# Decode attention, four layers: V15's second half in a bank of its own, wo columns ahead of V15, wq of layers 2 and 3 in 1, 2, 2 rows

## The chip, the cores and the metric

The kernel runs on one core of a Trainium2 chip. The metric is the device time of one launch in microseconds (us), lower is better. A profile shows one execution; its span leaves out about 1.8 us of the launch, so a span of 1984.0 us belongs to a time of 1985.8 us.

## The reference, cut to what matters

Four layers, blocks A, B, A, B. Each normalises a vector of 640, projects it with wq (640 x 6144) to 32 heads of 192, attends over a cache of 8192 keys, projects with wo and adds the result to the vector. One query only, so every byte of the caches and weights is used once in a layer (layers 0 and 2 share theirs, and so do 1 and 3).

```python
    x = x + _A_ref(_layernorm(x, axis=-1), A_k_cache, A_v_cache, A_wq, A_wo)
    x = x + _B_ref(_layernorm(x, axis=-1), B_k_cache, B_v_cache, B_wq, B_wo)
    x = x + _A_ref(_layernorm(x, axis=-1), A_k_cache, A_v_cache, A_wq, A_wo)
    x = x + _B_ref(_layernorm(x, axis=-1), B_k_cache, B_v_cache, B_wq, B_wo)
# within a block: q = x @ wq; scores = q.k / sqrt(192); p = softmax; o = p @ v; out = o @ wo
```

## The kernel before

Heads go in 16 pairs per layer. K and V of a pair are 12.6 MB between them, and SBUF holds eight slots of 3.15 MB. For K, DVE multiplies the tile by the query and PE sums over the head dimension with the identity; for V, PE multiplies by the probabilities and DVE picks the wanted parts out of PSUM. A transfer into a slot is issued when the last reader of that slot is done. V15 stands for the V tile of the last pair of a layer, whichever pair that is.

The parts the change touches: which slices of wq come in which piece, how many of wo's 15 columns come late (`NB`, one number per layer), the order of the steps at a layer's end, and the V product.

```python
    Q_PARTS = [(0, 2), (2, 2), (4, 1)]        # first row and number of rows of each piece of wq
    NB = [0, 5, 0, 5]                         # wo columns that come after V15
    # ... (cut)
            steps.append(("e", l, p - 1))
            steps += [("v", l, p, 0), ("wc", l, 2)] if NB[l] else [("wc", l, 2), ("v", l, p, 0)]
            steps += [("wo", l, 2), ("v", l, p, 1)]
            if NB[l]:
                plan.append(("vq", l))
                both(("wob", l))
            steps.append(("e", l, p))
            both(("wol", l))
```

Here "v" is the V product, "e" the picks, "wc" the turning of 15 columns of the attention output, "wo" and "wob" the projections with the early and the late columns of wo, "wol" the last pair's projection, and "vq" the transfer of V15's last quarter. V15 has 2 keys per PSUM group, so that 2 picks instead of 8 follow it:

```python
                k = 2 if p == NPAIR - 1 else VK   # VK = 8
                # ... (cut)
                for i in range(2 if end else VK):
                    e = DV.op(lambda v, i=i: (
                        v.tensor_scalar(acc[:], O[:, 0:DH], pick[:, 0:1], None, ALU.mult) if i == 0 else
                        v.scalar_tensor_tensor(out=acc[:], in0=O[:, i * DH:(i + 1) * DH], scalar=pick[:, i:i + 1], in1=acc[:],
                                               op0=ALU.mult, op1=ALU.add)), e if i else None, bank=Ou)
```

In the step into layer 2 the slots chain: wq's third piece takes the slot of wq's first piece, and layer 2's first V half takes the slot of the first half of K0, which was kept since layer 0. So V is issued when PE has summed that K half, and that needs layer 2's first query.

## Time and profile before

| | before |
|---|---|
| median of the first 3 runs | 1985.51 us (1985.11 to 1985.80) |
| span of the profiled execution | 1984.0 us |
| bytes moved | 849.25 MB |
| slice 21 of 40 (the step into layer 2) | 388 GB/s |
| last slice | 353 GB/s |

How to read it: with transfers busy all the time, only places where the DMA engines stand still, and what follows the last transfer, can be won.

Besides the views, the trace records when each of a transfer's sixteen parts landed, and when each packet started and how long it took. "Landing" below means the last of the sixteen parts, and "spread" the distance from the first part to the last.

### The profile page before, as it was taken

Reading aid. Unit: us, or ns where it says so; the run is one execution under the profiler, and the core shown is the slowest. Engines: PE = TensorE matmul, PEld = TensorE weight load, DVE = VectorE, ACT = ScalarE, POOL = GpSimd, SP = SyncE. Lnnn points to the kernel's source line nnn. Section 1 sums busy time; section 2 is a strip of 40 time slices with the busy share of each in tenths; the row PEclk is TensorE's granted clock in tenths of the full one; section 3 lists DMA queues with packets and bytes.
Section 4 is the critical chain, followed back from the end, with each engine's and each line's share of the span. In section 5 each row is a group of like instructions: output and inputs, shape, how many; then the busy total and the mean of one; then the engine's idle time right before and its main releaser. Section 6 shows DMA issues by size and latency. Waiting matters only on the chain.

```text
span 1984.0 us, 13908 instructions
## 1 busy us (share of the span) xinstructions
PE 1273.4 (64%) x8310; PEld 150.1 (8%) x3266; DVE 1200.7 (61%) x1371; ACT 139.5 (7%) x461; POOL 4.5 (0%) x22
## 2 busy tenths in 40 slices
PE   3567567566466666665775665675676766656657
PEld 0001001000200100100020010010002001001001
DVE  3566467467166656556745565665664775665665
ACT  0000000000000000000010000000000000000000
POOL 0000000000000000000000000000000000000000
PEclk9787777777587787777876777878886887777777
DMA  9999999999999999999999999999999999999998
GB/s 412 438 430 431 431 437 429 431 430 431 433 435 431 432 429 436 430 431 432 427 388 433 430 430 430 432 430 430 431 431 427 435 432 434 430 432 432 432 431 353
DMA packets 26926, 849.25 MB, mean 428 GB/s; under 512 B 3184, under 2 KB 3184, under 8 KB 3952
## 3 DMA queue, kind: packets, MB, share of 16 engines
q1 hardware_dynamic: 26720, 848.38, 99.5%
q8 instruction: 45, 0.74, 0.2%
q14 instruction: 17, 0.14, 0.0%
q10 hardware_dynamic: 144, 0.00, 0.0%
HBM read 848.36 MB, written 0.00 MB: 428 GB/s over the span
## 4 chain that ended last, share of the span: by engine, by line
DMA 68%; DVE 15%; PE 15%; ACT 1%; issue 0%; SPq 0%
DMA pool<-in_B_k_cache_dram 27%; DMA pool<-in_A_v_cache_dram 20%; DMA pool<-in_A_k_cache_dram 14%; DVE pool L543 13%; PE S L58 6%; PE OY L58 5%; DMA pool<-in_B_v_cache_dram 4%; PE OY L620 3%; DMA pool<-in_B_wo_dram 2%; ACT p_sb L580 1%; DVE acc L639 1%; DMA pool<-in_A_wq_dram 1%; DVE s_sb L565 1%; PE OY L513 0%; PE S L556 0%
## 5 line engine op out<-in xcount | busy, mean ns | idle before, releaser
L543 DVE TENSOR_TENSOR pool<-pool,q_sb 128x3072 bf16<-128x3072 bf16 x512 | 861.2, 1753 | 241.5 <-DMA pool<-in_B_k_cache_dram 144.0
L58 PE MATMUL S<-pool,ident 128*128 128x512 bf16 x2944 | 789.1, 425 | 20.3 <-DVE pool L543 19.0
L650 PE MATMUL TB<-acc,small 128*1 128x192 f32 x240 | 82.1, 493 | 219.1 <-DVE acc L639 219.1
L556 PE MATMUL S<-pool,ident 128*128 128x512 bf16 x128 | 62.9, 491 | 213.6 <-DVE pool L543 213.6
L58 PE MATMUL OY<-pool,p_sb 128*16 128x512 bf16 x1920 | 197.0, 485 | 0.0
L638 DVE TENSOR_SCALAR acc<-OY,small 128x192 f32<-128x192 f32 x64 | 26.7, 418 | 274.2 <-PE OY L58 246.2
L620 PE MATMUL OY<-pool,p_sb 128*16 128x512 bf16 (+1 forms) x1216 | 147.5, 497 | 62.7 <-DMA pool<-in_A_v_cache_dram 56.4
L639 DVE SCALAR_TENSOR_TENSOR acc<-OY,small,acc 128x192 f32<-128x192 f32 x424 | 177.1, 418 | 14.9
L565 DVE TENSOR_REDUCE s_sb<-S 128x64 f32<-128x512 f32 x128 | 88.1, 688 | 69.4 <-PE S L58 69.4
L502 ACT ACTIVATE q_sb<-QM 128x192 bf16<-128x192 f32 x60 | 19.9, 331 | 954.8 <-PE QM L496 954.8
L661 ACT ACTIVATE rows<-TB,small 1x192 bf16<-1x192 f32 x120 | 43.2, 406 | 585.1 <-PE TB L650 585.1
L634 DVE RECIPROCAL small<-TB 1x2 f32<-1x2 f32 x64 | 11.2, 175 | 96.7 <-PE TB L595 75.2
L580 ACT ACTIVATE p_sb<-s_sb,small 64x128 bf16<-64x128 f32 x128 | 55.7, 435 | 161.9 <-DVE small L574 161.1
L556 PEld LDWEIGHTS S<-pool,ident 128*128 128x128 bf16 x128 | 13.0, 101 | 686.2 <-DVE pool L543 636.4
L595 PE MATMUL TB<-small,ones 128*1 128x2 f32 x120 | 11.4, 165 | 74.1 <-ACT p_sb L580 74.1
L620 PEld LDWEIGHTS OY<-pool,p_sb 128*16 128x16 bf16 (+1 forms) x1216 | 39.3, 107 | 203.6 <-issue 133.5
L570 PE MATMUL QM<-ident,m_bf 128*64 128x64 bf16 x128 | 14.1, 217 | 54.4 <-DVE m_bf L567 53.8
L650 PEld LDWEIGHTS TB<-acc,small 128*1 128x1 f32 x240 | 19.7, 101 | 311.4 <-DVE acc L639 283.9
L513 PE MATMUL OY<-oT,pool 128*128 128x1 bf16 x900 | 38.2, 178 | 3.5 <-ACT oT L528 2.8
L513 PEld LDWEIGHTS OY<-oT,pool 128*128 128x128 bf16 x900 | 37.1, 131 | 7.0 <-ACT oT L528 3.6
L574 DVE TENSOR_REDUCE small<-QM 128x1 f32<-128x64 f32 x64 | 14.4, 225 | 36.1 <-PE QM L570 36.1
L496 PEld LDWEIGHTS QM<-rows,one_b 1*64 1x64 bf16 x120 | 6.2, 100 | 350.7 <-issue 344.8
(59 smaller groups left out, 186.1 us busy)
## 6 DMA issues: line engine op xcount, KB each, us to landing
pool<-in_B_k_cache_dram SPq DMA_DIRECT2D x28, 6144.0 KB, 38.1
pool<-in_B_v_cache_dram SPq DMA_DIRECT2D x28, 6144.0 KB, 34.2
pool<-in_A_v_cache_dram SPq DMA_DIRECT2D x27, 6144.0 KB, 27.6
pool<-in_A_k_cache_dram SPq DMA_DIRECT2D x34, 3072.0 KB, 20.4
pool<-in_A_k_cache_dram SPq DMA_DIRECT2D x14, 6144.0 KB, 36.8
pool<-in_A_v_cache_dram SPq DMA_DIRECT2D x10, 3072.0 KB, 14.3
pool<-in_B_k_cache_dram SPq DMA_DIRECT2D x8, 3072.0 KB, 22.7
pool<-in_A_wo_dram SPq DMA_DIRECT2D x6, 2400.0 KB, 21.4
```

Of the source, the lines that this page charges most:

```text
L58: return t.add_instruction(mybir.InstMatmult(name=t.bass.get_next_instruction_name(), engine=mybir.EngineType.PE, ins=[t.lower_ap(rhs), t. ...
L502: lambda a: a.activation(q_sb[i][:], QM[:, 0:DH], ACT.Copy), e, last["q"][i], bank=QMu)
L513: e = PE.op(lambda t, i=i, c=c, f=y_first[0], fin=n[0] == "wol" and i == k - 1: t.matmul(YB[:, c:c + 1], lhsT=t3[:, i, c:D:DC], rhs=o[:, i ...
L543: e = DV.op(lambda v, d0=d0: v.tensor_tensor(k3[:, :, d0:d0 + QD], kin[:, :, d0:d0 + QD], q_sb[qi][:, d0:d0 + QD].unsqueeze(1).broadcast_t ...
L556: t.matmul(S[:, :], lhsT=ident[:], rhs=k3[:, :, d0:d0 + R], start=True, stop=fin) if d0 == 0 else
L565: lambda v, u=u: v.tensor_reduce(s[:, u * JU:(u + 1) * JU], SP_[u][:].rearrange("p (j r) -> p j r", r=R), AX.X, ALU.add), ev_S[p, u], last ...
L580: ev_p[p] = AC.op(lambda a, h=h, r=r: a.activation(p_sb[par][r, :, h], s[r, :], ACT.Exp, bias=negm[par][r, 0:1], accum_out=l_col[par][r, h ...
L620: t.matmul(o, lhsT=x, rhs=y, start=f, stop=fin) if c == 0 else
L638: v.tensor_scalar(acc[:], O[:, 0:DH], pick[:, 0:1], None, ALU.mult) if i == 0 else
L639: v.scalar_tensor_tensor(out=acc[:], in0=O[:, i * DH:(i + 1) * DH], scalar=pick[:, i:i + 1], in1=acc[:], op0=ALU.mult, op1=ALU.add)), e if ...
L650: e = PE.op(lambda t, h=h: t.matmul(TB[96:97, C_O + h * DH:C_O + (h + 1) * DH], lhsT=half[:, h:h + 1], rhs=acc[:], start=True, stop=True), ...
L661: last["TO"] = last["row_written"] = AC.op(lambda a, h=h: a.activation(orow[:, o0 + h * DH:o0 + (h + 1) * DH], TB[96:97, C_O + h * DH:C_O ...
```

## The change

The intent: at the end of layers 1 and 3, let V15's first half be summed and picked (8 keys per group) while the second half is still on its way, and put the second half into the free scores bank with 2 keys per group, so that only two picks follow it; turn the output's columns before V15, not in its middle; bring fewer wo columns late; and issue wq in pieces that give its first slot back sooner. The first query's copy also goes from ACT to DVE.

```diff
-    Q_PARTS = [(0, 2), (2, 2), (4, 1)]
+    Q_PARTS = [[(0, 2), (2, 2), (4, 1)] if l < 2 else [(0, 1), (1, 2), (3, 2)] for l in range(NL)]
-    NB = [0, 5, 0, 5]
+    NB = [0, 0, 0, 3]
+    SPLIT = (1, 3)
...
-            steps += [("v", l, p, 0), ("wc", l, 2)] if NB[l] else [("wc", l, 2), ("v", l, p, 0)]
-            steps += [("wo", l, 2), ("v", l, p, 1)]
+            steps.append(("wc", l, 2))
+            if l in SPLIT:
+                steps += [("v", l, p, 0), ("e", l, p, 0), ("wo", l, 2), ("v", l, p, 1)]
+                plan.append(("vq", l))
+            else:
+                steps += [("wo", l, 2), ("v", l, p)]
...
-            ev_q[0] = last["QB"] = AC.op(
-                lambda a: a.activation(q_sb[i0][:], QM[:, 0:DH], ACT.Copy, scale=rs[:, 0:1]),
+            ev_q[0] = last["QB"] = DV.op(
+                lambda v: v.tensor_scalar(q_sb[i0][:], QM[:, 0:DH], rs[:, 0:1], None, ALU.mult),
...
-                k = 2 if p == NPAIR - 1 else VK
+                k, B, Bu = (2, SP_[0], Su[0]) if part == 1 else (VK, O, Ou)
...
+                for i in range(2 if part == 1 else VK):
                     e = DV.op(lambda v, i=i: (
-                        v.tensor_scalar(acc[:], O[:, 0:DH], pick[:, 0:1], None, ALU.mult) if i == 0 else
-                        v.scalar_tensor_tensor(out=acc[:], in0=O[:, i * DH:(i + 1) * DH], ...
+                        v.tensor_scalar(acc[:], O[:, 0:DH], pick[:, 0:1], None, ALU.mult) if i == 0 and part != 1 else
+                        v.scalar_tensor_tensor(out=acc[:], in0=B[:, i * DH:(i + 1) * DH], ...
```

The cuts leave out how the events and slot releases of the two halves are kept apart.

More of the change, by code (lines that the diff above doesn't have):

```diff
@@ L265, in build @@
             steps.append(("e", l, p - 1))
-            steps += [("v", l, p, 0), ("wc", l, 2)] if NB[l] else [("wc", l, 2), ("v", l, p, 0)]
-            steps += [("wo", l, 2), ("v", l, p, 1)]
+            steps.append(("wc", l, 2))
[4 more added lines that the diff above has]
+                steps += [("wo", l, 2), ("v", l, p)]
             if NB[l]:
-                plan.append(("vq", l))
                 both(("wob", l))
@@ L280, in released @@
                     l, p = l + 2, ORDER[l + 2]["pairs"].index(pair(l, p))
-                return at[("v", l, p, 1) if n[0] == "v" and p == NPAIR - 1 else ("v", l, p) if n[0] == "v" else ("m", l, p, n[3])]
+                return at[("v", l, p, n[3]) if n[0] == "v" and p == NPAIR - 1 and l in SPLIT else ("v", l, p) if n[0] == "v" else ("m", l, p, n[3])]
             return at[("wob", n[1]) if n[0] == "wo" and n[2] == 2 and NB[n[1]] else n]
@@ L325, in wq_rows @@
         def wq_rows(l, g):
-            c0, k = Q_PARTS[g]
+            c0, k = Q_PARTS[l][g]
             if l < 2:
@@ L333, in quarters @@
         def quarters(n):
-            return n[0] == "v" and n[2:] == (NPAIR - 1, 1) and NB[n[1]] > 0
+            return n[0] == "v" and n[2:] == (NPAIR - 1, 1) and n[1] in SPLIT
         def transfer(n):
@@ L374, in transfer @@
             elif n[0] == "wq":
-                c0, k = Q_PARTS[n[2]]
+                c0, k = Q_PARTS[l][n[2]]
                 f = lambda s: s.dma_start(
@@ L405, in build @@
                     lc=[None, None], S=[None, None], O=ev_zero)
-        for k in "MX QB rows qbc TT TO YB orow oT oTl acc rl xb rs st stt row_written".split():
+        for k in "MX QB rows qbc TT TO YB orow oT oTl acc rl xb rs st stt sel row_written".split():
             last[k] = None
@@ L469, in q_rows @@
                 n = ("wq", l, g)
-                c0, k = Q_PARTS[g]
+                c0, k = Q_PARTS[l][g]
                 t3 = wq_rows(l, g)[:, :, ORDER[l]["q1"] * PD if l < 2 else 0:]
@@ L583, in softmax, with values @@
                 last["s"][par] = last["negm"][par] = ev_p[p]
-            def values(p, us=(0, 1)):
+            def values(p, part=None):
                 par = (l * NPAIR + p) % 2
                 nl, np_ = first_load("v", l, p)
-                k = 2 if p == NPAIR - 1 else VK
-                N = min(512, k * DH)
                 PE.wait(ev_p[p])
-                if 0 in us:
+                if part != 1:
                     PE.wait(last["rl"])
@@ L602, in values @@
                     last["lc"][par] = ev_l[p] = e
-                PE.wait(last["O"])
-                rounds = J // k // G
-                for r in range(us[0] * rounds // 2, (us[-1] + 1) * rounds // 2):
-                    u, i = divmod(r, rounds // 2)
-                    u = turn[nl, np_][u]
+                k, B, Bu = (2, SP_[0], Su[0]) if part == 1 else (VK, O, Ou)
+                PE.wait(last["S"][0] if part == 1 else last["O"])
+                N = min(512, k * DH)
+                groups = []
+                for u in (turn[nl, np_] if part is None else (part,)):
+                    groups += [(u, j) for j in range(0, JU, k)]
+                n = len(groups)
+                for r in range(0, n, G):
+                    u, j = groups[r]
                     PE.wait(need(("v", nl, np_, u)))
+                    if part == 1 and j >= JU // 2:
+                        PE.wait(need(("vq", l)))
                     t = slot[place[("v", nl, np_, u)]]
-                    if p == NPAIR - 1 and i == rounds // 4 and quarters(("v", nl, np_, u)):
-                        PE.wait(need(("vq", l)))
                     for c in range(k * DH // N):
                         for g in range(G):
-                            j = (i * G + g) * k
-                            o, x, y = (O[32 * g:32 * g + 2 * k, c * N:(c + 1) * N],
+                            u, j = groups[r + g]
+                            o, x, y = (B[32 * g:32 * g + 2 * k, c * N:(c + 1) * N],
                                        p_sb[par][:, u * JU + j:u * JU + j + k, :].rearrange("p j h -> p (j h)"),
                                        t[:, j * DH + c * N:j * DH + (c + 1) * N])
-                            f, fin = r == 0, r == rounds - 1
+                            f, fin = r == 0, r == n - G
                             e = PE.op(lambda t, c=c, g=g, o=o, x=x, y=y, f=f, fin=fin: (
@@ L621, in values @@
                                 matmul_held(t, o, x, y, f, fin, 32, 32 * g)),
-                                signal=(fin and c == k * DH // N - 1 and g == G - 1), bank=Ou)
-                if 1 not in us:
-                    return
-                ev_O[p] = last["p"][par] = e
+                                signal=(fin and c == k * DH // N - 1 and g == G - 1), bank=Bu)
+                ev_O[p, part] = last["p"][par] = e
                 if not stays("v", l, p):
-                    for u in range(2):
+                    for u in ((0, 1) if part is None else (part,)):
@@ L628, in values, with select @@
                         freed[("v", nl, np_, u)] = e
+            def select(p, part=None):
+                end = p == NPAIR - 1
+                a, n = (slice(0, P), 1) if end else (slice(96, 97), 2)
+                if part != 1:
+                    last["rl"] = DV.op(lambda v: v.reciprocal(rl[a, 0:n], TB[a, C_L:C_L + n]), ev_l[p], last["TO"], bank=TBu)
+                DV.wait(ev_O[p, part], last["acc"], ev_pick)
+                e = None
+                B, Bu = (SP_[0], Su[0]) if part == 1 else (O, Ou)
+                for i in range(2 if part == 1 else VK):
+                    e = DV.op(lambda v, i=i: (
+                        v.tensor_scalar(acc[:], O[:, 0:DH], pick[:, 0:1], None, ALU.mult) if i == 0 and part != 1 else
+                        v.scalar_tensor_tensor(out=acc[:], in0=B[:, i * DH:(i + 1) * DH], scalar=pick[:, i:i + 1], in1=acc[:],
+                                               op0=ALU.mult, op1=ALU.add)), e or last["sel"], bank=Bu)
+                if part == 1:
+                    last["S"][0] = e
+                else:
+                    last["O"] = e
+                last["sel"] = e
+                return e
@@ L630, in gather @@
             def gather(p):
                 end = p == NPAIR - 1
-                a, n = (slice(0, P), 1) if end else (slice(96, 97), 2)
-                ev_rl = last["rl"] = DV.op(lambda v: v.reciprocal(rl[a, 0:n], TB[a, C_L:C_L + n]), ev_l[p], last["TO"], bank=TBu)
-                DV.wait(ev_O[p], last["acc"], ev_pick)
-                for i in range(2 if end else VK):
-                    e = DV.op(lambda v, i=i: (
-                        v.tensor_scalar(acc[:], O[:, 0:DH], pick[:, 0:1], None, ALU.mult) if i == 0 else
-                        v.scalar_tensor_tensor(out=acc[:], in0=O[:, i * DH:(i + 1) * DH], scalar=pick[:, i:i + 1], in1=acc[:],
-                                               op0=ALU.mult, op1=ALU.add)), e if i else None, bank=Ou)
@@ L641, in gather @@
-                last["O"] = e
+                e = select(p, 1 if end and l in SPLIT else None)
+                ev_rl = last["rl"]
                 PE.wait(e, last["TO"], last["TT"])
@@ L671, in layer @@
                 elif n[0] == "v":
-                    values(n[2], n[3:] or (0, 1))
+                    values(*n[2:])
                 elif n[0] == "e":
-                    gather(n[2])
+                    (select if n[3:] else gather)(*n[2:])
                 elif n[0] == "wq":
```

## The prediction

> **What bounds the kernel now.** I read the page's 40 slices first, then its chain by engine, then the chain in order of time, then the busy shares of short stretches around the two places where the slices dip.
>
> ```profile
> DMA  9999999999999999999999999999999999999998
> GB/s 412 438 430 431 431 437 429 431 430 431 433 435 431 432 429 436 430 431 432 427 388 433 430 430 430 432 430 430 431 431 427 435 432 434 430 432 432 432 431 353
> DMA packets 26926, 849.25 MB, mean 428 GB/s; under 512 B 3184, under 2 KB 3184, under 8 KB 3952
> ...
> DMA 68%; DVE 15%; PE 15%; ACT 1%; issue 0%; SPq 0%
> ```
>
> The transfers are busy in every slice, while PE and DVE are busy 64% and 61% of the span and hide behind them. In the undisturbed parts the trace moves 433 GB/s; 849.25 MB at that rate is 1961.3 us of a span of 1984.0. The change loads the same bytes. So everything any schedule could win is 22.7 us, 1.1%: **faster by 2% (39.7 us) is out of reach**. Two slices dip: number 21 (388, the step from layer 1 to layer 2) and the last (353, the end). Slice 21 lacks 45/433 x 49.6 = 5.2 us. Those are where the change works.
>
> How much of the dip counts? Each transfer lands in sixteen parts, one per DMA engine, and the trace has their landings. The first of the sixteen parts comes well before the last, and the distance grows: 1.25 us at 22 us, 3.8 us at 500 us, 6.5 us at 1002.85. Only the last part releases a consumer. So what counts is the engine that lags. While the fifteen others idle ahead of it, nothing is lost. From the last landings, with 7.30 us for a half tile of 3.15 MB (the usual distance):
>
> - 1002.85 first half of V15, 1006.54 and 1010.20 its second half, 1012.14 the late wo columns, 1013.32 the last wo rows, 1020.24 and 1027.14 wq with two rows each, 1030.59 wq with one row. All these distances are bytes over rate: the lagging engine never stops, though the slices dip around 1006 and 1024.
> - The next landing, the first V half of layer 2, is at 1039.25: 8.66 us after 1030.59 for a transfer of 7.30 us. **Here even the slowest engine stands still, 1.36 us.** Its first part lands at 1038.69, so all sixteen started together: all had been empty.
>
> ```profile
> 1022.00:1024.00 2.00, 2.00 (x17) 0.10 (x1) 2.00 (x2) 0.00 (x0) 0.00 (x0) 0.50 0.84 357
> 1024.00:1026.00 2.00, 2.00 (x9) 0.00 (x0) 2.00 (x2) 0.00 (x0) 0.00 (x0) 0.77 0.83 265
> 1026.00:1028.00 2.00, 2.00 (x11) 0.00 (x0) 2.00 (x2) 0.00 (x0) 0.00 (x0) 1.00 1.04 444
> 1028.00:1030.00 2.00, 2.00 (x17) 0.09 (x3) 2.00 (x2) 0.00 (x0) 0.00 (x0) 1.00 0.37 156
> ```
>
> Columns: stretch, length, busy PE, PE loads, DVE, ACT, POOL, granted PE clock, DMA share, GB/s. Only the last stretch is a real stop. The transfer that ends it was held back:
>
> ```profile
> 1007.03 16.99 SPq L376 DMA_DIRECT2D pool<-in_A_wq_dram  x3
> 1029.60 0.34 SPq L371 DMA_DIRECT2D pool<-in_A_v_cache_dram  x1
> ```
>
> The queue issues wq's three pieces from 1007.03 to 1024, then V at 1029.60, since V takes the place of K0's first half, whose products end only then: PE was in the queries of wq's first piece from 1020.28 to 1023.65, because that piece landed at 1020.24.
>
> The end of the span:
>
> ```profile
> 1937.57 40.13 DMA pool<-in_B_wo_dram
> 1977.70 0.05 issue
> 1977.74 1.16 PE OY L513 x25
> 1978.90 0.99 PE TB L646 x12
> 1979.89 0.02 issue
> 1979.91 0.28 ACT oTl L656
> 1980.19 0.04 issue
> 1980.23 0.77 PE OY L513 x15
> 1981.01 0.02 issue
> 1981.03 0.16 DVE x_bf L696
> ```
>
> The late wo columns land at 1977.70, 25 projections follow, then the turn of the last pair, its projection and the output. Beside it, DVE's second pick ended at about 1978.46: two paths within 0.4 us.
>
> **What the Trainium skill says.** "DMA: Bandwidth & Descriptors", section "Why a DMA increments its semaphore by 16 and not by 1": a transfer runs on up to sixteen engines that finish independently, and only the full count means landed. The trace agrees (spread up to 6.5 us). The same page, "Where 436 GB/s comes from", gives a ceiling of 435.2 GB/s; the trace's 433 leaves nothing to win in rate. "Runtime: NRT & Kernel Launch", "Instruction fetch mechanics": instructions come in blocks of 16 KiB through a DMA queue of their own. The trace has packets of 16384 B of about 1.05 us each, and the spread grows in steps of about 1 us; one more or fewer on the lagging engine is my noise. "TensorE: Matmul & The Clock Gate", "What's actually happening": the clock is halved until about 3.4 us of activity; here it is 0.50 until 1024 and 1.00 from 1026, some 5 us after PE resumed.
>
> **The change part by part.** The slots that every transfer gets come out the same when I follow both allotments; only release times move.
>
> 1. *wo whole in layer 1, ahead of V15.* The 5 late columns (1.94 us) move before V15; bytes equal. V15's last quarter lands at 1012.14 instead of 1010.20. After it: half of 32 products of 2.73 us, 1.37; two picks of 0.42 and hops, 0.95; so the turn of the last pair starts at 1014.45, against 1013.27. It **costs 1.2 us** on the path into layer 2: first query at 1019.75 instead of 1018.57 (its copy goes from ACT, 0.42 us, to DVE, about the same).
> 2. *wo columns ahead of V15.* The 15 column products (1.07 us) follow ACT's rows at 1001.8, not V15's first half: the last wo rows and wq are issued near 1003, 3.7 us earlier. wq's second piece, waiting on the wo slot, goes at 1010.6 instead of about 1013. This fills the leading engines only.
> 3. *wq in 1, 2, 2 rows.* The first piece lands at 1016.75 instead of 1020.24, before the state is normalised; its queries take half of 3.3 us, from 1019.3 to 1020.9. The third piece, which needs that slot, goes at 1020.9 instead of about 1023.7 and keeps the lagging engine busy until 1030.5. K0's first products are then bound by DVE: four chunks of 1.68 us from 1019.75, and 1.46 for the last six matmuls, 1028.0. **V is issued at 1028.0 instead of 1029.60, 1.6 us earlier.** Issue to slowest landing was 9.65 us, less 7.30 of transfer: 2.35 of fixed delay. So it could flow at 1030.35, with the engine free at 1030.5: the stop of 1.36 us closes, by a margin of about 0.2.
> 4. *V15's halves.* The first half with 8 keys per group is 24 matmuls of 512 columns instead of 32 of 384, 2.56 us at half clock instead of 2.73. Its 8 picks (0.42 + 3.14 us from the trace) lie beside wo's projection and the wait for the second half. The second half stays at 32 matmuls and 2 picks. Layers 0 and 2 take 8 keys throughout, 6 more picks, 2.6 us, at layer ends that have over 10 us of transfers issued ahead (landings there show no stop). Nothing on the path.
> 5. *The end.* wo with 12 columns delays V15 by 0.8 us: its last quarter lands at 1976.55, not 1975.77. PE is free in time now, where before it came 0.4 us late from the projection. Matmuls to 1977.95, picks to 1978.9, the turn at 1978.9 instead of 1978.83. wo's 3 columns, landed at 1977.7, need 0.7 and are done at 1978.65. **About +0.1 us.**
>
> Sum: -1.36 + 0.1 = -1.3 us. I add nothing for fewer PE instructions (about 190 of 11,576, under one fetch).
>
> **The rivals.**
> - *All of slice 21 comes back* (gaps at 1006, 1024 and 1029, some 4.9 us): then 1980.5. For it, the GB/s row; against it, the lagging engine, which shows no idle in the first two. It would need the lag to be harmless.
> - *The stop stays:* the clock rises later, or 1.2 us from part 1 eats the 1.6, and V is issued at 1029 or later. Then 0.4 to 1.3 us of it remain, 1984.5 to 1985.6. For it: a margin of 0.2 us. Against: PE begins 1 us earlier too.
> - *The tail gains:* the split takes picks off the path and ends 1 us earlier, 1983. Against it: two picks stay behind the last landing.
> - *The later layers lose,* by 6 more picks. DVE is off the path there; nothing.
>
> **Range and chances.** 1985.5 - 1.3 = 1984.2. From 1982.3 (a further 1 to 2 us from a fetch or the tail) to 1985.6 (nothing closes). Faster by over 2%: 0.003; within 2%: 0.994; slower: 0.003.
>
> **What would show it.** The distance between the landings of wq's third piece and of the first V half of layer 2 should fall from 8.66 to about 7.3 us; V's issue should come about 1.6 us earlier against wq's last landing; slice 21 should rise above 400 GB/s; the chain at the end should pass through a pick or the last quarter of V15 and not through 25 wo matmuls, with 7.5 us from the landing of V15's last quarter to the end of the span in place of 8.2. I am wrong if the whole dip comes back as time, or the tail moves by over 1 us.

## More of the kernel before

The instruction fetches are a queue of their own on the page. The lines are kind, packets, MB and share of the sixteen engines' span.

```profile
q1 hardware_dynamic: 26720, 848.38, 99.5%
q8 instruction: 45, 0.74, 0.2%
```

## The result, and the profile after

The changed kernel took **1986.89 us** (median of 4 runs, 1985.87 to 1988.34) against 1985.65 us before (4 runs). The ratio is 1.0007, with a 95% interval of 0.9990 to 1.0024: the same within 2%, but above the predicted range and on the other side of the kernel before. A ratio here is the mean time of one kernel's fast runs over the mean of the other's fast runs of the same rounds, so it isn't quite the ratio of the medians.

The page of the changed kernel, in the same rows as before (transfers, rate, packets, chain by engine):

```profile
DMA  9999999999999999999999999999999999999997
GB/s 412 436 432 429 430 437 429 430 437 425 434 436 430 429 435 432 429 432 435 425 398 438 423 420 431 431 427 430 434 429 427 436 428 434 433 432 433 431 434 340
DMA packets 26782, 849.25 MB, mean 428 GB/s; under 512 B 3168, under 2 KB 3168, under 8 KB 3808
...
DMA 65%; PE 17%; DVE 16%; ACT 1%; issue 0%; SPq 0%
```

Slice 21 went from 388 to 398 only, not above 400, and the two slices after it fell from 433 and 430 to 423 and 420. The second trace of the same kernel (again, below) has 396 for slice 21 and 431 and 432 after it, so only the first of these is the kernel's own. The stretches of the step into layer 2 (same columns as in the prediction; DMA share and GB/s are the last two):

```profile
1020.00:1022.00 2.00, 1.38 (x9) 0.10 (x1) 2.00 (x2) 0.00 (x0) 0.00 (x0) 0.50 0.71 230
1022.00:1024.00 2.00, 2.00 (x7) 0.00 (x0) 2.00 (x2) 0.00 (x0) 0.00 (x0) 0.50 0.95 380
...
1028.00:1030.00 2.00, 2.00 (x27) 0.27 (x7) 2.00 (x2) 0.00 (x0) 0.00 (x0) 1.00 1.13 388
1030.00:1032.00 2.00, 2.00 (x11) 0.00 (x0) 2.00 (x2) 0.00 (x0) 0.00 (x0) 1.00 0.90 369
1032.00:1034.00 2.00, 2.00 (x11) 0.00 (x0) 1.19 (x2) 0.00 (x0) 0.00 (x0) 1.00 0.95 406
```

The same in the kernel before, from 1030 on:

```profile
1030.00:1032.00 2.00, 2.00 (x25) 0.19 (x4) 2.00 (x3) 0.00 (x0) 0.00 (x0) 1.00 0.78 209
1032.00:1034.00 2.00, 2.00 (x11) 0.00 (x0) 0.61 (x2) 0.00 (x0) 0.00 (x0) 1.00 1.06 455
```

The hole of 156 GB/s at 1028 is gone. Where before the rate is back at 430 and more from 1032 on, it now stays below 410 until 1036. And there is a new hole of 230 GB/s at 1020, where the kernel before had 444: the first parts of wq's second piece landed at 1019.47 us, and its third piece was issued only at 1020.39. The queue's issues (start, duration, queue, line):

```profile
1003.69 17.08 SPq L380 DMA_DIRECT2D pool<-in_A_wq_dram  x3
1028.12 0.34 SPq L375 DMA_DIRECT2D pool<-in_A_v_cache_dram  x1
```

V is issued at 1028.12, where the prediction had 1028.0. Yet it lands at 1040.05 us, later than before (1039.25), and 9.58 us after wq's third piece. Fifteen of its sixteen parts land within 0.81 us, and the sixteenth 1.95 us after those.

The chain at the end (start, duration, what):

```profile
1974.54 2.50 PE OY L517 x60
1977.03 2.69 PE S L626 x32
1979.74 0.43 DVE acc L646
1980.20 0.43 DVE acc L646
1980.63 0.04 issue
1980.67 0.91 PE TB L664 x12
1981.61 0.28 ACT oTl L674
1981.88 0.05 issue
1981.93 0.77 PE OY L517 x15
1982.72 0.16 DVE x_bf L714
```

It runs through V15's second half and its two picks, as predicted, and no longer through 25 wo matmuls. But V15's 32 matmuls follow 60 projections directly, though the last quarter had landed at 1977.77: PE, not the landing, holds the end. In the second trace it is the landing: the last quarter comes at 1976.10 us and PE takes it up at 1976.14.

### The profile page after: what moved, and what is told of

It is laid out like the page before. It is cut to its first block, busy times and chain, and to the rows that moved or that the text cites. A ratio compares the mean times of both kernels' runs of the same rounds, so it can differ in the third digit from the quotient of the medians.

```text
span 1985.9 us, 13752 instructions
## 1 busy us (share of the span) xinstructions
PE 1272.5 (64%) x8262; PEld 146.2 (7%) x3122; DVE 1213.7 (61%) x1403; ACT 137.7 (7%) x457; POOL 4.4 (0%) x22
## 2 busy tenths in 40 slices
DMA packets 26782, 849.25 MB, mean 428 GB/s; under 512 B 3168, under 2 KB 3168, under 8 KB 3808
## 4 chain that ended last, share of the span: by engine, by line
DMA 65%; PE 17%; DVE 16%; ACT 1%; issue 0%; SPq 0%
DMA pool<-in_B_k_cache_dram 26%; DMA pool<-in_A_v_cache_dram 22%; DVE pool L547 14%; DMA pool<-in_A_k_cache_dram 13%; PE S L58 7%; PE OY L58 5%; DMA pool<-in_B_v_cache_dram 4%; PE OY L626 3%; DVE acc L646 1%; DMA pool<-in_B_wq_dram 1%; ACT p_sb L584 1%; DVE s_sb L569 1%; PE OY L517 1%; PE S L560 0%; DVE m_bf L571 0%
## 5 line engine op out<-in xcount | busy, mean ns | idle before, releaser
L58 PE MATMUL OY<-pool,p_sb 128*16 128x512 bf16 x2016 | 212.5, 497 | 0.0
L646 DVE SCALAR_TENSOR_TENSOR acc<-OY,small,acc 128x192 f32<-128x192 f32 x448 | 187.1, 418 | 15.7
L626 PE MATMUL OY<-pool,p_sb 128*16 128x512 bf16 x1008 | 134.0, 499 | 69.9 <-DMA pool<-in_A_v_cache_dram 64.1
L626 PEld LDWEIGHTS OY<-pool,p_sb 128*16 128x16 bf16 x1008 | 34.0, 106 | 209.5 <-issue 129.8
```

What stands on the lines that cost most here:

```text
L58: return t.add_instruction(mybir.InstMatmult(name=t.bass.get_next_instruction_name(), engine=mybir.EngineType.PE, ins=[t.lower_ap(rhs), t. ...
L626: t.matmul(o, lhsT=x, rhs=y, start=f, stop=fin) if c == 0 else
L646: v.scalar_tensor_tensor(out=acc[:], in0=B[:, i * DH:(i + 1) * DH], scalar=pick[:, i:i + 1], in1=acc[:], op0=ALU.mult, op1=ALU.add)), e or ...
```

## The experiments

My theory after the first trace was that the change does what it was meant to up to V's issue, and that the time goes where the DMA engines start again after they have run dry; the open question was whether that start is late because of an instruction fetch, because of luck, or because it always costs. The rival was that the change itself (its picks, its PE order) costs time somewhere else.

Eleven runs of 5 timed executions each were made, in three batches on three chips, each batch with nine executions of the kernel before (means 1986.26, 1985.79 and 1985.92 us). For each trace, four numbers are read the same way: when V of layer 2 was issued; how long before the landing of wq's third piece that was ("lead"); the distance from that landing to V's; and the median time of this V's first sixteen packets of 24,576 B. (The trace names no engine for a packet, so I take these for the first packets of the sixteen engines; an early engine's second packet can be among them.) The first two rows are the kernels of the change.

| kernel | V issued | lead | distance | first packet | time, mean of runs |
|---|---|---|---|---|---|
| before | 1029.60 | 0.99 | 8.66 | 1.54 | 1985.94 (31) |
| changed | 1028.12 | 2.36 | 9.58 | 1.33 | 1987.00 (4) |
| again | 1028.14 | 1.82 | 8.45 | 1.47 | 1987.88 (5) |
| wq_old | 1028.78 | 1.64 | 10.63 | 1.57 | 1988.11 (5) |
| pe_dose | 1030.47 | 1.01 | 8.82 | 1.52 | 1988.73 (5) |
| after_phase | 1027.85 | 2.77 | 9.13 | 1.30 | 1987.04 (5) |
| before_phase | 1028.18 | 1.86 | 8.88 | 1.48 | 1986.09 (5) |
| late13_delay | 1029.07 | 2.49 | 8.67 | 1.55 | 1987.25 (5) |
| only_wq | 1027.39 | 3.45 | 7.29 | 0.92 | 1985.73 (5) |
| only_wq2 | 1026.51 | 4.59 | 7.34 | 0.94 | 1985.37 (5) |
| late1 | 1026.42 | 4.34 | 7.31 | 1.08 | 1986.67 (5) |
| late13 | 1026.19 | 4.47 | 7.36 | 0.98 | 1986.17 (5) |
| late_both | 1027.39 | 4.20 | 7.30 | 0.99 | 1986.01 (5) |

The time of the kernel before is the mean of all its 31 runs; their standard deviation is 0.86 us, so a mean of 5 is good to about 0.4 us, and to 0.7 us where a kernel scatters more (wq_old, 1.6 us). Only larger differences are read from times. The distance sorts the traces better, though there is one trace a run: it is 7.29 to 7.36 us in five and 8.45 us or more in eight, with nothing between. Slice 21 of the page sorts them alike: 402 to 407 GB/s in the five, 398 or less in the eight. But the distance isn't itself a cost, since wq's landing moves too: again's V lands at 1038.41 us, 0.84 us before that of the kernel before.

### again: the changed kernel once more

No edit.

> The changed kernel once more, for more samples of its time. Theory (fetches): the 2 us that the first profiled run lost come from an instruction fetch of 16 KiB that met one DMA engine just as it started again at the step into layer 2, and from how many such fetches fall on the engine that lags; both are luck of the execution, so this run has V of layer 2's first half landing 7.3 us after wq's third piece in some executions and 9.6 us in others, and times between 1984 and 1988.5 us. Rival (the change itself costs): every execution has the late landing, and the time is 1.2 us above the kernel before in all rounds.

Measured: 1987.78 us median, 1986.48 to 1989.63; the kernel before 1985.94 in the same rounds; ratio 1.0008 (0.9995 to 1.0021). In this trace V lands 8.45 us after wq's third piece and the spread is 0.89 us, so the late engine of the first trace doesn't come in every execution. (One or two late parts do come again below, in wq_old, after_phase, before_phase and late13_delay.) The rest stayed: fifteen parts land 9.2 to 10.0 us after the issue in the first trace and 9.4 to 9.8 in this one, against 9.1 to 9.6 in the kernel before. A fetch of 16,384 B starts at 1028.85 us in the first trace and at 1029.15 in this one, that is, in both traced restarts of the changed kernel. That made the fetch the first suspect. With both sets of runs the changed kernel's mean is 1987.49 us (9 runs), 1.55 us above the kernel before; of the two expectations, the rival's (1.2 us, in every execution) came nearer.

### only_wq and wq_old: one part alone, and the change without it

only_wq is the kernel before with this edit, and wq_old is the changed kernel with it undone:

```diff
-    Q_PARTS = [(0, 2), (2, 2), (4, 1)]
+    Q_PARTS = [[(0, 2), (2, 2), (4, 1)] if l < 2 else [(0, 1), (1, 2), (3, 2)] for l in range(NL)]
```

> The kernel before with one part of the change: wq of layers 2 and 3 in 1, 2, 2 rows. Theory: this part alone issues V of layer 2 earlier than 1029.60 us (its queries of one row take 1.6 us less and wq's first piece lands 3.4 us earlier) and so closes most of the 1.36 us stop; distance of the two landings 7.3 to 7.8 us, time 0.5 to 1.4 us below the kernel before unless fetches hide it. Rival (the part moves nothing that sets the end): distance stays at 8.7 us, time within 0.3 us.

> The changed kernel with wq of layers 2 and 3 in 2, 2, 1 rows as before. Theory: the stop at the step into layer 2 comes back, and grows, as V15's later landing starts that layer 1.2 us later: distance of the two landings 9 to 10 us, time 1 to 2.5 us above the changed kernel. Rival: no difference beyond 0.5 us.

Measured: only_wq 1985.41 us median (1985.30 to 1986.34), ratio 0.9997 (0.9985 to 1.0010); wq_old 1988.57 (1985.81 to 1989.86), ratio 1.0009 (0.9997 to 1.0022). The distance is 7.29 us in only_wq and 10.63 us in wq_old. The part by itself issues V 2.2 us earlier than before, since V15 isn't put off by wo's columns, and the stop closes altogether. These are only_wq's stretches of the restart:

```profile
1028.00:1030.00 2.00, 2.00 (x23) 0.12 (x4) 2.00 (x3) 0.00 (x0) 0.00 (x0) 1.00 1.14 461
1030.00:1032.00 2.00, 2.00 (x11) 0.00 (x0) 2.00 (x2) 0.00 (x0) 0.00 (x0) 1.00 1.07 460
1032.00:1034.00 2.00, 2.00 (x11) 0.00 (x0) 0.11 (x1) 0.00 (x0) 0.00 (x0) 1.00 1.00 430
```

None of these three is below 400 GB/s. only_wq's time is 0.5 us below the kernel before in the same rounds, as expected but within the noise. wq_old missed: its distance is above the expected 9 to 10 us, and its mean lies 0.6 us above the changed kernel's, and 0.2 us above again's in the same rounds, where 1 to 2.5 was expected. The noise can't tell that from its rival, no difference.

### pe_dose: more instruction fetches

Thirty spare one-column matmuls ahead of every half tile's products, in the kernel before:

```diff
                 PE.wait(last["S"][u], ev_const)
+                for i in range(30):
+                    PE.op(lambda t, i=i: (
+                        t.matmul(S[:, 0:1], lhsT=ident[:], rhs=ident[:, 0:1], start=True, stop=True) if i == 0 else
+                        matmul_held(t, S[:, 0:1], ident[:], ident[:, 0:1], True, True)), signal=False, bank=Su[u])
```

> The kernel before with 30 spare one-column matmuls ahead of each of 128 half tiles' products, about 3,970 more PE instructions, in time that PE spends waiting for DVE's first chunk. Theory (fetches load the DMA engines that bound the kernel): 15 to 16 more packets of 16384 B, 1.05 us each on one engine, fall mostly on nine engines, so the lagging engine gains about 1.7 of them: span 1.5 to 3.5 us longer, the spread of the sixteen landings at 1000 us up from 6.5 to 8 us or more. Rival (fetches are hidden): time within 0.5 us, spread unchanged.

Measured: 1988.40 us median (1987.79 to 1990.23), 2.5 us above the kernel before; ratio 1.0013 (0.9999 to 1.0026). The queue of PE's instructions grew as expected:

```profile
q8 instruction: 61, 1.00, 0.2%
```

So 16 more fetches came, and the time is within the expected 1.5 to 3.5 us. The spread was a miss: at 996 us it is 7.15 us against some 6.5 before, and 5.3 to 5.8 soon after, not 8 or more. And not all of the time is the fetches': V was also issued 0.87 us later, as the spare matmuls took 28 ns each, and lands 1.04 us later. From V's landing to that of the last wo rows it was 940.97 us against 939.61, 1.4 us more for the same bytes and 7 more fetches. That is in keeping with fetches that cost DMA time, but a single trace of each doesn't settle it: late13_delay, below, has no more fetches there than the kernel before and took 941.34 us.

### after_phase and before_phase: the fetch moved off the restart, and towards it

Spare instructions as above, but in layer 0 only, 32 per half tile (31 matmuls and a load): 96 in the changed kernel, as many as the change took out of layers 0 and 1, and 160 in the kernel before.

```diff
+                for i in range(31 if l == 0 and u == 0 and 1 <= p <= 3 else 0):   # 5 in before_phase
```

> The changed kernel with 96 spare one-column PE instructions in layer 0 (pairs 1 to 3, while PE waits for DVE), which makes up for the 96 PE instructions that the change took out of layers 0 and 1, so PE's instruction fetches fall at the same places of the program as before. Theory (a fetch at the restart): no fetch within 5 us of 1028, the one there moves to about 1018.7 us, the first V half of layer 2 lands at most 9.7 us after its issue and its sixteen parts within 1.0 us, and the time falls by 0.5 to 2 us against the changed kernel, to 1985.0 to 1986.5. Rival (luck of the engines alone): the time stays at about 1987.5, and the lagging engine at the restart comes and goes as before.

> The kernel before with 160 spare one-column PE instructions in layer 0, 160 being 256 less 96, so its fetches fall where the changed kernel has them. Theory (a fetch at the restart): a fetch of 16384 B near 1029 to 1031 us, one of the sixteen parts of the first V half of layer 2 0.4 to 2.7 us behind the others, time 0.5 to 2 us above the kernel before. Rival (160 PE instructions cost nothing): time within 0.3 us of the kernel before.

Measured: after_phase 1986.89 us median (1986.17 to 1987.87), mean 0.45 us below the changed kernel's; before_phase 1986.15 (1984.62 to 1986.89), mean 0.15 us above. The fetch moved: in after_phase none starts between 1019.42 and 1058.22 us. In before_phase one is at 1026.05, over before V's issue and not at 1029 to 1031 as intended, so that run tests little; its mean is 0.3 us above the kernel before's in the same rounds, as far as its rival went. But after_phase's V still lands 9.13 us after wq's third piece, with two parts 1.66 and 2.42 us after the first. So **the theory of a fetch at the restart falls**: without one, the restart is as slow. late_both, below, has a fetch at 1029.03 and no slow restart; late13_delay has none from 1018.69 to 1046.05 and a slow one.

### late1 and late13: late wo columns again

The changed kernel with after_phase's 96 instructions and, in the one, 5 late columns in layer 1; in the other, 5 in layer 3 as well.

```diff
-    NB = [0, 0, 0, 3]
+    NB = [0, 5, 0, 3]     # late1;  [0, 5, 0, 5] in late13
```

> The changed kernel with 5 late wo columns in layer 1 again (3 in layer 3), and the 96 spare PE instructions. Theory (the stop at the step into layer 2 is the length of the chain from V15's last landing to V's issue): V15 of layer 1 lands 1.9 us earlier, V of layer 2 is issued 1.0 to 1.9 us earlier than in the changed kernel with the same 96, the distance of its landing from wq's third piece falls from about 8.4 to 7.3 us, and the time by 0.5 to 1.2 us. Rival (wq's second piece, which has to wait for the late columns again, becomes the wait): distance unchanged, time within 0.3 us.

> As the last, and with 5 late wo columns in layer 3 too, where the change has 3. Theory (the end is PE's chain and not the landing): V15 of layer 3 lands 0.76 us earlier, its last matmuls end about 0.4 us earlier as PE projects 10 columns fewer ahead of them, and the end after K15's landing is 0.1 to 0.4 us shorter than with 3. Rival (landing bound, 25 late projections take the place): no shorter, or up to 0.3 us longer.

Measured: late1 1986.64 us median (1985.46 to 1988.11), late13 1985.94 (1985.32 to 1987.20). In layer 1, V15 lands at 1009.88 us instead of 1011.93 (after_phase), V is issued 1.43 us earlier, and the distance falls from 9.13 to 7.31 us: the theory holds in each number of the trace, while the gain in time, 0.37 us, is below the noise. The step of late13 is smaller than any noise: from K15's landing to PE's end 38.93 us against 39.05. From the landing of the last wo rows to PE's end it is 2.13 us, as before, and 2.17 in late1.

### late13_delay: V's issue put off

late13 with 65 spare matmuls (1.8 us) ahead of the last six of K0's first half in layer 2, into the other scores bank.

```diff
                     PE.wait(chunks[c])
+                    if l == 2 and p == 0 and u == 0 and c == 3:
+                        PE.wait(last["S"][1])
+                        for i in range(65):
+                            PE.op(lambda t: matmul_held(t, SP_[1][:, 0:1], ident[:], ident[:, 0:1], True, True),
+                                  signal=False, bank=Su[1])
```

> The changed kernel with 5 late columns in layers 1 and 3 and the 96 spare PE instructions, and 65 spare one-column matmuls (28 ns each, 1.8 us) ahead of the last six matmuls of K0's first half in layer 2, which put V's issue off from 1026.2 to about 1028.0 us, 2.5 us before wq's third piece has landed. Theory (an engine that has run dry starts again late, and slower in its first packet): the distance of the two landings goes from 7.36 to between 8.4 and 10 us, and the time up by 0.8 to 2.5 us. Rival (my prediction's model: a fixed delay of 2.35 us after the issue, and only the lagging engine counts): V could flow at 1030.4, the lagging engine is free at 1030.3, so the distance stays at 7.3 to 7.5 us and the time within 0.3 us.

Measured: 1987.37 us median (1986.00 to 1988.77), mean 1.1 us above late13's. The issue came at 1029.07 us, 2.49 us before wq's third piece landed; the distance is 8.67 us. My model would have had V flow at 1029.07 + 2.35 = 1031.4, before the landing at 1031.56, hence a distance near 7.3. This is the run that decides: its edit puts off the issue and leaves the transfers as they are, and the restart became slow. Three things limit it. The 1.1 us of time is hardly clear of the noise. The issue came 2.88 us later than late13's, 1.8 of it by the edit. And fifteen of the sixteen parts land within 7.30 us of wq's third piece; the distance is that of one part, 1.37 us behind them.

```profile
1028.00:1030.00 2.00, 2.00 (x22) 0.18 (x6) 2.00 (x2) 0.00 (x0) 0.00 (x0) 1.00 0.71 300
1030.00:1032.00 2.00, 2.00 (x19) 0.10 (x1) 2.00 (x3) 0.00 (x0) 0.00 (x0) 1.00 1.14 366
```

The packets show what the restart is. In late13, 4 of V's first 16 packets take more than 1.2 us; here 12 do, with a median of 1.55 us, where the packets after it take 0.91. In the changed kernel it is 10, in the kernel before 14.

### late_both and only_wq2: versions that might beat both

late_both is the changed kernel with `NB = [0, 5, 0, 5]` and nothing else; only_wq2 is only_wq again.

> The changed kernel with 5 late wo columns in layers 1 and 3 as the kernel before has them, without spare instructions. Theory (the two places where the change moved wo columns ahead of V15 are what it loses by): V of layer 2 is issued near 1026.3, the distance of the landings is 7.3 to 7.4 us, PE ends 2.1 to 2.2 us after the last wo rows land, and the time is 0.8 to 1.8 us below the changed kernel's mean of 1987.5, level with or up to 0.8 us below the kernel before. Rival (the split of V15 and its picks lose as well): 0.5 us or more above the kernel before.

> The kernel before with wq in 1, 2, 2 rows alone, once more, for a closer mean beside the last. Theory: distance of the landings 7.3 us again, time 0.2 to 1.2 us below the kernel before. Rival (its five runs of before were luck): the distance is over 8 us in this trace, time level with the kernel before or above it.

Measured: late_both 1985.95 us median (1985.73 to 1986.42), ratio 1.0000 (0.9988 to 1.0013), 1.5 us below the changed kernel's mean and level with the kernel before, as expected. V was issued at 1027.39 us, 1.1 us later than expected, and the restart was quick all the same. only_wq2 1985.26 (1984.87 to 1986.30), ratio 0.9997 (0.9984 to 1.0011). The end of late_both:

```profile
1977.61 1.16 PE OY L517 x25
1978.77 0.99 PE TB L664 x12
1979.76 0.02 issue
1979.78 0.27 ACT oTl L674
```

It is the end of the kernel before again: the late wo columns set it, 25 of them, and the split of V15 and its picks are off the path and gain nothing. `NB` is all that sets it apart from the changed kernel, so moving these columns ahead of V15 is what lost the time; the times don't part layer 1's share from layer 3's. Over its ten runs only_wq has a mean of 1985.55 us, against 1985.94 over 31 runs of the kernel before: it is the best that ran, but 0.4 us isn't clear of the noise. All runs gave correct results.

## Why the prediction was right or wrong, point by point

- **The bound, and no 2%**: right. The same 849.25 MB at the same rate, and all thirteen means lie within 0.2% of each other.
- **Part 1, wo whole in layer 1, "costs 1.2 us"**: right, and too kindly judged. V15 landed at 1011.39, the turn of the last pair began at 1013.86 instead of 1013.27, 0.6 us later (that execution's V15 landed 0.75 us sooner than I had it). Without this part V is issued 1.4 us earlier (late1 against after_phase). It was the part that decided the outcome, since it took the lead that the restart needed.
- **Part 2**: right; the last wo rows and wq went out at 1003.3 and 1003.7.
- **Part 3, to V's issue**: right to 0.1 us (1028.12 for 1028.0), by luck. V15's earlier landing started K0's products at 1019.16 us instead of 1019.75; from there to V's issue it took 8.96 us instead of 8.25. The sum had these products bound by DVE, but PE at half clock fell behind: DVE's fourth chunk ended at 1025.92, and PE's matmuls, half-clocked until about 1024.6, only at 1028.09. In after_phase and late13, where the clock rose at 1023.6 and 1022.0, it was 8.30 us.
- **The step that failed** is the next one of part 3: "2.35 of fixed delay. So it could flow at 1030.35, with the engine free at 1030.5: the stop of 1.36 us closes". The delay isn't fixed. With the measured issues and landings of wq's third piece that sum gives a distance of 7.30 us in the first trace of the changed kernel and 7.83 in the second; it was 9.58 and 8.45. From issue to the slowest landing it was 9.65 us before, but 10.27 and 11.93 in the two traces of the changed kernel. I had reasoned "while the fifteen others idle ahead of it, nothing is lost", and that is wrong when they run dry. Their first packets then take 1.3 to 1.6 us in the median instead of 0.9 to 1.1, and in five of the eight slow traces one or two engines begin so late, or take so long over a packet, that they become the lagging ones (in the first trace one begins at 1031.22 us, the others by 1030.13, and its packet takes 2.12 us). The spread at wq's third piece had shrunk to 1.24 and 0.67 us in the changed kernel, but it doesn't decide: it was 2.21 us in late13_delay, which is slow, and 1.58 in late1, which isn't. What parts the traces is the lead: 2.77 us or less in every slow one, 3.45 or more in every quick one. That it is the first engines to run dry that set this border is my reading: counted to the landing of wq's first part, the lead was 1.72 us in after_phase (slow) and 1.70 in late_both (quick).
- **In numbers**: the sum had -1.36 us for the stop. In its place V landed 0.80 us later (first trace) and 0.84 us earlier (again) than before.
- **Part 4**: right as far as it goes; nothing of it was on the path, and late_both shows no gain from it.
- **Part 5, about +0.1 us**: right in kind, a little small. From the last wo rows' landing to PE's end it was 2.13 us before, 2.58 and 2.29 in the changed kernel. In the first trace PE was late, with V15's last 32 matmuls straight after 60 projections, where I had put PE as free in time. The sign of 7.5 us from the last quarter's landing to the end of the span failed: it was 8.15 and 8.31, against 8.25 before. In the second trace 0.65 us of that lies in the output's own transfer, which landed 3.06 us after its issue instead of 2.41.
- **The rivals**: "the stop stays" came nearest, and one of its two reasons was at work, unseen: the clock rose late enough to hold PE back by 0.7 us. V15's early landing made up for it, so V was issued in time, and even so the restart was slow. "All of slice 21 comes back" was far off, and "the tail gains" too.
- **The range**: its top was "nothing closes". It had no room for a restart that costs more than the stop it follows, nor for the noise: the kernel before alone ran from 1984.43 to 1988.58 us in its later rounds.

What stays open: the changed kernel's mean is 1.55 us above the kernel before, and its two traces account on average for less than half of that. In the first PE ended 1.69 us later than before (0.80 by V's landing, 0.45 from there to the last wo rows' landing, 0.45 at the end), in the second 0.26 us earlier (-0.84, 0.42 and 0.16). From V's landing to that of the last wo rows, with the same bytes, the thirteen traces differ by 1.8 us (939.58 to 941.34), and the changed kernel's lie in the middle (940.06 and 940.03, against 939.61). I put this scatter down to which engines the fetches meet, and it was only argued: one trace per kernel can't separate it from another cause.

## What to carry to other kernels

In a kernel bound by transfers, a gap must be closed with time to spare: it was not enough that the next transfer was issued before the slowest engine was done. Here it had to go out some 3 us ahead of the last landing, before the fast engines ran dry, as I read it. Trace the chain that sets that issue and take work off it, rather than moving bytes; the one part of the change that shortened it (wq's first piece with one row) did better alone (1985.55 us) than together with the part that lengthened it again (1987.49). And before a gain below 0.1% is believed, run the old kernel often enough to know its own scatter.

## What the Trainium skill lacked or had wrong

- "DMA: Bandwidth & Descriptors" (section "Latency and other measured facts") gives about 600 ns to the first byte for transfers issued from SP. Here, with the engines empty, the first packet began 0.98 us after the issuing instruction began in the kernel before (1029.60 to 1030.58), which is 0.64 us after its end, so the figure agrees if it counts from there. The first packets then took 1.54 us in the median instead of 0.91. No page tells of that, or that a single engine can start 1 to 2 us after the others (one part of 16 landed 1.95 us after the rest in the changed kernel).
- The same page says that the engines of one transfer finish independently, but not by how much: here the spread grew to 6.5 us over 1000 us of unbroken transfers.
- "Runtime: NRT & Kernel Launch" (section "Instruction fetch mechanics") calls the cost of a 16 KiB boundary "mostly hidden". Its block size agrees (45 packets of 16,384 B for 11,576 PE instructions and loads, about 256 each). Each packet takes about 1.05 us of a DMA engine; whether that is hidden in a kernel bound by transfers isn't shown here. With 7 more fetches in the second half it took 1.4 us more (pe_dose), but late13_delay, with none more, took 1.7 us more than the kernel before (one trace each).
- At 1010 us seven of the sixteen parts land within 1.3 us of the first and nine 3.3 us or more after it, in the kernel before; 1.7 and 3.0 us in the changed one. That looks as if fetches fell on nine engines only; no page says which engines serve them, and no run here settles it.
